# Attention beside two MLPs on one core: the low part of the row maxima by way of PSUM, and the broadcast of reciprocal sums in two transfers

## The chip, the cores and the metric

One core of a Trainium2 chip runs the whole program. The metric is the device time of one execution in microseconds (us), the median of several runs. A core has TensorE (PE, matrix products), VectorE (DVE), ScalarE (ACT), GpSimd (POOL) and SyncE (SP, which issues DMA transfers). SBUF is the large on-chip memory; PE writes its results to PSUM.

## The reference

Three parts in a row: causal attention with a position bias for 4 batches of 8 heads (576 tokens, 64 columns each), a dense MLP, and a mixture of eight experts with capacity. The change touches attention alone:

```python
scores = scale * np.matmul(q, k.transpose(0, 1, 3, 2))
s_pos = np.maximum(s, 0.0)
cum = np.cumsum(s_pos, axis=-1)
bias = -(cum[:, :, :, None] - cum[:, :, None, :])
scores = np.where(causal, -1000000000.0, scores + np.minimum(bias, 0.0))
scores = scores - np.max(scores, axis=-1, keepdims=True)
attn = np.exp(scores)
attn = attn / (np.sum(attn, axis=-1, keepdims=True) + 1e-09)
return np.matmul(attn, v).astype(np.float32)
```

Then follow `x @ w_in`, a piecewise quadratic function, `@ w_out`; and top-1 routing of 2304 tokens to eight experts of 288 tokens, each `relu(x @ w1) @ w2`.

## The kernel before, in words

The order of the work is written by hand: each engine carries out its instructions in the order in which the program issues them.

**Attention** (class `Attention`) goes through 32 heads, two of which make a pair; an even and an odd head differ in what is prepared beside them. `run` (L383) does for head n: the maxima of the rows (`rows_max`, L236), the product of the previous head's weights with its values (`values`, L313), the scores again, transposed, with their exponentials (`exps`, L275), and pieces of the preparation of the next pair (`prep_hi`, `prep_lo`) and of the normalization of earlier pairs (`norm`, L361).

**The row maxima.** `rows_max` computes scores in six tiles of PSUM (tag "s", four buffers) by two matmuls each (L249, L250), and VectorE takes the negated maximum of each row (L252 with the causal mask, L256 without) into `mc`, 128 rows by five columns. The matmuls work on numbers of reduced precision, so every operand is split into a high part and a remainder. For the maxima this is `nm`: L258 casts `mc` to the high part, L259 subtracts it from `mc`, which gives the low part. `rows_put` (L262) transposes both on PE (L271, five small matmuls), and ScalarE copies them as two rows into the operand Z (L272); by these rows the second score product subtracts the maximum before the exponential. `rows_put` is called in the midst of `values` of the previous head: six values matmuls (L333) stand ahead of L271 on PE, four behind it, then the scores of `exps` (L301).

**Normalization.** V has a column of ones, so `values` yields the sums of the weights too. `sums` (L354) lays them out as 128x9, and `norm` goes in five steps: 0 adds 1e-9 and takes the reciprocals (L369, L370), 1 writes them to DRAM (`rd`, L372), 2 reads them back as a tile R in which 64 partitions for each of the pair's two heads hold the same 576 numbers (L375), 3 multiplies (L378), 4 stores (L381). The steps of a pair lie in heads after it: step 2 of a pair stands in one odd head, step 3 in the next odd head. The transfers are issued from GpSimd's queue (`self.q`); after attention, for the last pairs, from SP's.

**Beside it** VectorE, ScalarE and GpSimd convert the first MLP's weights, which come as 64-bit floats in two 32-bit words, in every head (`narrow`, L486): VectorE takes the words apart (L495, L496, L501, L503), ScalarE converts (L499, L505), and GpSimd multiplies mantissa by exponent, two tiles in SBUF of 128x512 (L506). SP loads q, k and v for pairs to come (L187, L189, L178) and the raw weights (L514, L518).

**After attention** come the dense MLP (`Ffn`), routing (`Route`) and the experts (`Experts`). The first iterations of the MLP take weights that were converted before and carry out the last steps of `norm`.

Of the kernel before, what the change touches and what calls it, by code (L numbers as in the profile page):

```python
# [18 lines left out]
OP = mybir.AluOpType  # L19
# [5 lines left out]
def f(t):  # L25
    return t.bitcast(F32)
# [7 lines left out]
class Attention:  # L34
# [201 lines left out]
    def rows_max(self, n, fill):  # L236
        nc = self.nc
        X, Y, Z, W = self.stacks[(n // 2) % 2]
        h = n % 2
        mc = self.mcol[n % 2]  # L240
        for i, c0, c1, col in ((4, 0, 320, 5), (4, 320, 576, 4), (3, 0, 448, 3), (2, 0, 320, 2),
                               (1, 0, 192, 1), (0, 0, 64, 0)):
            if i == 1:
                fill()
            t = self.ps.tile([128, 512], F32, name="ps", tag="s", bufs=4)
            a, b = self.QT[i]
            m, w = b - a, c1 - c0
            diag = c1 == b
            nc.tensor.matmul(t[:m, :w], X[:, h, a:b], Y[:, h, c0:c1], start=True, stop=False)  # L249
            nc.tensor.matmul(t[:m, :w], Z[:96, h, a:b], W[:96, h, c0:c1], start=False, stop=True)  # L250
            if c1 == b:
                nc.vector.tensor_tensor_reduce(t[:m, :w], t[:m, :w], self.ml[:m, 448 + m - w:448 + m], -1.0,  # L252
                                               mc[:m, 5:6] if i == 4 else 3e38, op0=OP.add, op1=OP.min,
                                               accum_out=mc[:m, col:col + 1])
            else:
                nc.vector.tensor_reduce(mc[:m, col:col + 1], t[:m, :w], axis=AX.X, op=OP.max, negate=True)  # L256
        nm = self.w.tile([128, 5, 2], F32R, name="nm")
        nc.vector.tensor_copy(nm[:, :, 0], mc[:, :5])  # L258
        nc.vector.tensor_tensor(nm[:, :, 1], mc[:, :5], f(nm)[:, :, 0], op=OP.subtract)  # L259
        return nm  # L260

    def rows_put(self, n, nm):  # L262
# [98 lines left out]
    def norm(self, p, step):  # L361

        if not 0 <= p < self.NP:
            return
        nc, S = self.nc, self.S
        u0, r9, x = self.done[p]
        n = 2 * p
        if step == 0:
            nc.vector.tensor_scalar(r9, r9, 1e-9, None, op0=OP.add)  # L369
            nc.vector.reciprocal(r9, r9)  # L370
        elif step == 1:
            self.q.dma_start(self.rd[n:n + 2].rearrange("h (p s) -> (h p) s", p=64), r9)  # L372
        elif step == 2:
            R = self.nw.tile([128, S], F32, name="R")
            self.q.dma_start(R, self.rd[n:n + 2, None, :].to_broadcast([2, 64, S]))  # L375
            self.done[p] = (u0, r9, R)
        elif step == 3:
            nc.vector.tensor_tensor(x, u0, x, op=OP.mult)  # L378
        else:
            b, hh = divmod(n, self.H)  # L380
            self.q.dma_start(self.xd[64 * hh:64 * hh + 128, b * S:(b + 1) * S], x)  # L381
# [1278 lines left out]
```

## Time and profile before

| what | value |
|---|---|
| median of 3 runs | 1036.65 us (1034.18 to 1041.91) |
| the profiled execution | 1032.85 us |
| its span in the trace | 1031.1 us, mean granted TensorE clock 0.981 |
| instructions | 18509 |
| attention | about 14 to 292 us of the span |

The profile is of one execution. Times are counted from the start of the span. Engines are busy with instructions of the program; DMA issues on an engine's queue are rows of the order of time too (SPq is SP's queue), and of the source of a line. PEld is the load of weights into PE, which runs beside PE. Matmuls are pipelined, so a row can begin before the one ahead of it ends. A row of the order of time is: start, length, engine, line, operation, output and inputs, shapes, number; in brackets the idle time of its engine before it and what ended it. A row that sums a stretch has the length, the busy time of PE, PEld, DVE, ACT and POOL with the number of instructions in brackets, the granted TensorE clock, the busy share of the 16 DMA engines, and what they moved in GB/s. In a source row, three numbers are the shortest, the median and the longest of one instruction in ns.

### The profile page before, as it was taken

How to read it: one execution, taken by the hardware profiler on the slowest of the kernel's cores; microseconds unless marked ns; L12 is line 12 of the kernel's file. 1: busy time of each engine (PE TensorE's matmuls, PEld its weight loads, DVE VectorE, ACT ScalarE, POOL GpSimd, SP SyncE). 2: the span in 40 equal slices, each digit the busy share in tenths (PEclk: the TensorE clock that was granted, in tenths of full speed). 3: DMA queues.
4: the chain of work that ended last, by engine and by line, in shares of the span. 5: the costliest groups of instructions: out<-in, count | busy, mean ns of one | idle time of the engine just before them, and what ended most of it. 6: DMA issues, size and time to landing. Idle time of an engine off the chain costs nothing.

```text
span 1031.1 us, 18509 instructions
## 1 busy us (share of the span) xinstructions
PE 964.3 (94%) x6479; PEld 854.7 (83%) x6479; DVE 768.1 (74%) x2109; ACT 490.2 (48%) x961; POOL 338.8 (33%) x391
## 2 busy tenths in 40 slices
PE   6899999999979999999999999999889978989995
PEld 5777777777767989899889898899789868979995
DVE  6688888878857669799999998875568777775410
ACT  5777777767745542332332323430345424546431
POOL 3144454534421000000000000330778858873211
PEclk9999999999989999999999999999999989999998
DMA  5768777776667140030121300102555436557300
GB/s 130 161 165 194 200 201 191 200 194 173 189 203 246 54 147 29 21 102 22 31 93 31 113 11 11 62 11 81 159 165 172 157 115 190 165 147 222 118 24 24
DMA packets 124347, 126.86 MB, mean 123 GB/s; under 512 B 74178, under 2 KB 90818, under 8 KB 124124
## 3 DMA queue, kind: packets, MB, share of 16 engines
q1 hardware_dynamic: 104604, 89.79, 30.7%
q0 software_dynamic: 18592, 34.75, 11.6%
q10 hardware_dynamic: 1056, 1.12, 0.4%
q8 instruction: 51, 0.84, 0.3%
q14 instruction: 44, 0.36, 0.1%
HBM read 93.55 MB, written 27.50 MB: 117 GB/s over the span
## 4 chain that ended last, share of the span: by engine, by line
PE 58%; DVE 24%; DMA 5%; issue 5%; ACT 5%; POOL 1%; SPq 1%; another core or an unknown queue 0%; POOLq 0%; ACTq 0%; DVEq 0%
PE py L1493 8%; PE ph L1441 8%; PE ph L620 8%; PE po L333 6%; PE pst L301 6%; DVE junk L682 6%; PE px L661 3%; PE px L663 3%; PE px L662 3%; ACT u L629 3%; PE ps L249 2%; PE ps L250 2%; DVE u L628 2%; DVE gl L642 2%; PE rp L1128 2%
## 5 line engine op out<-in xcount | busy, mean ns | idle before, releaser
L1219 POOL TENSOR_TENSOR wl<-raw,wh 128x512 fp32r<-128x512 f32 x98 | 129.2, 1345 | 57.7 <-DMA raw<-in_moe_w_dram 33.8
L629 ACT ACTIVATE u<-u,half 128x384 f32<-128x384 f32 x96 | 59.3, 617 | 173.8 <-DVE u L628 169.0
L620 PE MATMUL ph<-xh,ih 128*128 128x384 f32 x384 | 130.8, 341 | 3.6 <-ACT ih L584 3.6
L620 PE MATMUL ph<-xh,il 128*128 128x384 f32 x384 | 130.6, 340 | 0.2 <-DVE il L592 0.2
L620 PE MATMUL ph<-xl,ih 128*128 128x384 f32 x384 | 130.5, 340 | 0.0
L333 PE MATMUL po<-E,V 128*128 128x320 f32 (+4 forms) x448 | 113.9, 383 | 0.4 <-ACT E L305 0.4
L663 PE MATMUL px<-oh,gl 128*128 128x512 f32 x240 | 95.3, 397 | 3.7 <-DVE gl L642 3.7
L661 PE MATMUL px<-oh,gh 128*128 128x512 f32 x240 | 95.2, 397 | 1.9 <-ACT x L670 1.8
L662 PE MATMUL px<-ol,gh 128*128 128x512 f32 x240 | 94.5, 394 | 0.0
L333 PEld LDWEIGHTS po<-E,V 128*128 128x128 f32 (+1 forms) x448 | 75.9, 194 | 20.5 <-issue 7.8
L682 DVE SCALAR_TENSOR_TENSOR junk<-x,gb 128x512 f32<-128x512 f32 x120 | 84.9, 737 | 4.5 <-ACT x L670 4.5
L682 DVE SCALAR_TENSOR_TENSOR junk<-wt,gb 128x512 f32<-128x512 f32 x128 | 82.9, 685 | 0.0
L1493 PE MATMUL py<-hh,wh 128*128 128x288 f32 x256 | 81.0, 317 | 0.0
L1219 ACT ACTIVATE wh<-raw 128x512 fp32r<-128x512 f32 x128 | 75.9, 624 | 9.2 <-DMA raw<-in_moe_w_dram 8.0
L1441 PE MATMUL ph<-xh,wh 128*128 128x288 f32 x256 | 79.4, 310 | 0.4 <-ACT xh L1219 0.4
L1441 PE MATMUL ph<-xl,wh 128*128 128x288 f32 x256 | 79.0, 309 | 0.5 <-DVE xl L1219 0.4
L620 PEld LDWEIGHTS ph<-xh,ih 128*128 128x128 f32 x384 | 72.7, 189 | 8.0 <-ACT ih L584 3.9
L1441 PE MATMUL ph<-xh,wl 128*128 128x288 f32 x256 | 78.4, 306 | 0.0
L1493 PE MATMUL py<-hl,wh 128*128 128x288 f32 x256 | 77.5, 303 | 0.0
L1493 PE MATMUL py<-hh,wl 128*128 128x288 f32 x256 | 77.2, 302 | 0.0
L620 PEld LDWEIGHTS ph<-xl,ih 128*128 128x128 f32 x384 | 72.7, 189 | 3.4
L506 POOL TENSOR_TENSOR co<-cm,ce 128x512 f32<-128x512 f32 x32 | 40.5, 1264 | 104.2 <-ACT cm L505 99.4
(228 smaller groups left out, 2487.9 us busy)
## 6 DMA issues: line engine op xcount, KB each, us to landing
raw<-in_moe_w_dram SPq DMA_DIRECT2D x128, 256.0 KB
r<-in_moe_w_in_dram SPq DMA_DIRECT2D x16, 512.0 KB
r<-in_moe_w_out_dram SPq DMA_DIRECT2D x16, 512.0 KB
xg<-xd SPq DMA_DIRECT2D x6, 768.0 KB
x2d<-x SPq DMA_DIRECT2D x36, 128.0 KB
Y<-Y POOLq DMA_DIRECT2D x15, 288.0 KB
nk<-in_k_dram SPq DMA_DIRECT2D x32, 128.0 KB
nq<-in_q_dram SPq DMA_DIRECT2D x32, 128.0 KB
```

What stands on the lines that cost most here:

```text
L301: nc.tensor.matmul(pst[u][:, cols], l, r, start=first, stop=last, skip_group_check=u == "c" or u == "b")
L333: nc.tensor.matmul(t[:, 256 + c0:256 + g1], V[:b - a, kb, 64 * h:64 * h + 128], E[:b - a, e0:e0 + g1 - c0], start=i == 0, stop=i == len(or ...
L506: nc.gpsimd.tensor_tensor(out, f(m), f(e), op=OP.mult)
L620: nc.tensor.matmul(p[:, :G], a[:, s], b, start=n == 0, stop=n == 11)
L629: nc.scalar.activation(u, u, AF.Square, bias=self.half, scale=0.5)
L661: nc.tensor.matmul(px[t][:, cols], gh[:, s], oh[:, cols], start=i == 0, stop=False)
L662: nc.tensor.matmul(px[t][:, cols], gh[:, s], ol[:, cols], start=False, stop=False)
L663: nc.tensor.matmul(px[t][:, cols], gl[:, s], oh[:, cols], start=False, stop=last)
L682: self.nc.vector.scalar_tensor_tensor(junk, x(), 1.0, self.gb[:, e], op0=OP.mult, op1=OP.mult, accum_out=out[:, e:e + 1])
L1219: return fn(*a, **kw)
L1441: self.nc.tensor.matmul(p[:, :self.C], a[:, cols], b, start=c == 0 and i == 0, stop=c == 3 and i == 2)
L1493: nc.tensor.matmul(p[:, :C], a[:, o:o + 128], b[:, fb], start=fb == 0 and i == 0, stop=fb == 7 and i == 2)
```

## The change

Two edits. In `rows_max`, `mc` is copied to five unused columns of the last score tile in PSUM, and the subtraction that yields the low part reads `mc` from there. In step 2 of `norm`, the one transfer with the source [2, 64, 576] becomes two with the source [64, 576], one for each head, to the two halves of R's partitions.

```diff
@@ -256,7 +256,10 @@
         nm = self.w.tile([128, 5, 2], F32R, name="nm")
         nc.vector.tensor_copy(nm[:, :, 0], mc[:, :5])
-        nc.vector.tensor_tensor(nm[:, :, 1], mc[:, :5], f(nm)[:, :, 0], op=OP.subtract)
+
+
+        nc.vector.tensor_copy(t[:, 256:261], mc[:, :5])
+        nc.vector.tensor_tensor(nm[:, :, 1], t[:, 256:261], f(nm)[:, :, 0], op=OP.subtract)
         return nm
 
     def rows_put(self, n, nm):
@@ -372,7 +375,9 @@
         elif step == 2:
             R = self.nw.tile([128, S], F32, name="R")
-            self.q.dma_start(R, self.rd[n:n + 2, None, :].to_broadcast([2, 64, S]))
+
+            for h in range(2):
+                self.q.dma_start(R[64 * h:64 * h + 64], self.rd[n + h:n + h + 1, :].to_broadcast([64, S]))
             self.done[p] = (u0, r9, R)
```

## Rows read from the trace of the kernel before

**Rows 1.** The page, busy time, share of the span and instructions of each engine.

```profile
PE 964.3 (94%) x6479; PEld 854.7 (83%) x6479; DVE 768.1 (74%) x2109; ACT 490.2 (48%) x961; POOL 338.8 (33%) x391
```

**Rows 2.** By stretch: length, busy PE, PEld, DVE, ACT, POOL, clock, DMA share, GB/s.

```profile
234.25:242.75 8.50, 7.78 (x53) 6.16 (x53) 8.13 (x21) 6.25 (x13) 5.19 (x7) 1.00 0.83 206
242.75:251.12 8.37, 8.37 (x56) 6.78 (x55) 6.42 (x22) 6.56 (x14) 2.85 (x5) 1.00 0.74 187
206.25:217.18 10.93, 9.04 (x54) 7.33 (x53) 6.54 (x22) 7.37 (x14) 2.59 (x5) 0.87 0.60 165
```

**Rows 3.** Order of time, an odd head: around the maxima's low part.

```profile
233.17 1.86 PE L333 MATMUL po<-E,V 128*128 128x320 f32 x6
...
234.25 0.17 DVE L258 CAST nm<-m 128x5 fp32r<-128x5 f32 x1
234.41 1.26 POOL L506 TENSOR_TENSOR co<-cm,ce 128x512 f32<-128x512 f32 x1 [4.11 <-ACT cm L505]
234.46 1.24 DVE L259 TENSOR_TENSOR nm<-m,nm 128x5 fp32r<-128x5 f32 x1
...
235.75 0.52 PE L271 MATMUL pr<-identr,nm 64*2 64x64 f32 x5 [0.72 <-DVE nm L259]
```

**Rows 4.** Order of time, an earlier odd head: the same instructions.

```profile
44.40 1.86 PE L333 MATMUL po<-E,V 128*128 128x320 f32 x6
...
45.68 0.17 DVE L259 TENSOR_TENSOR nm<-m,nm 128x5 fp32r<-128x5 f32 x1
45.69 1.29 POOL L506 TENSOR_TENSOR co<-cm,ce 128x512 f32<-128x512 f32 x1 [4.72 <-issue]
...
46.19 0.52 PE L271 MATMUL pr<-identr,nm 64*2 64x64 f32 x5
```

**Rows 5.** Order of time, an even head: low part and transposes.

```profile
242.95 0.17 DVE L259 TENSOR_TENSOR nm<-m,nm 128x5 fp32r<-128x5 f32 x1
...
243.87 0.52 PE L271 MATMUL pr<-identr,nm 64*2 64x64 f32 x5
```

**Rows 6.** Order of time, VectorE: first and last of 12 long subtractions.

```profile
61.76 1.24 DVE L259 TENSOR_TENSOR nm<-m,nm 128x5 fp32r<-128x5 f32 x1
...
268.20 1.24 DVE L259 TENSOR_TENSOR nm<-m,nm 128x5 fp32r<-128x5 f32 x1
```

**Rows 7.** Source of L259, and who on PE waited for it (us, times).

```profile
L259 DVE TENSOR_TENSOR nm<-m,nm x32: 165/167/1251, 14.5 to 284.4; 128x5 fp32r<-128x5 f32 x32
...
  PE pr L271: 9.6, 13
```

**Rows 8.** Groups by line and shape: small VectorE operations that read PSUM.

```profile
L737 DVE COPY L<-plt 128x24 f32<-128x24 f32 x1 | 0.2, 182 | 1.6 <-PE plt L735 1.6
...
L252 DVE CUSTOM_DVE_ANT_0 ps<-ps,ml 64x64 f32<-64x64 f32 x32 | 8.2, 255 | 0.0
```

**Rows 9.** Order of time, another odd head: GpSimd, a masked maximum, the cast.

```profile
216.68 1.26 POOL L506 TENSOR_TENSOR co<-cm,ce 128x512 f32<-128x512 f32 x1 [5.82 <-ACT cm L505]
...
216.83 0.26 DVE L252 CUSTOM_DVE_ANT_0 ps<-ps,ml 64x64 f32<-64x64 f32 x1
...
217.18 0.79 DVE L258 CAST nm<-m 128x5 fp32r<-128x5 f32 x1
```

**Rows 10.** Source of L375: GpSimd's issues of the broadcast.

```profile
L375 POOL DMA_DIRECT2D R<-rd x14: 835/848/1072, 65.8 to 288.0; - x14
```

**Rows 11.** By stretch, the MLP's begin: loads, then one of SP's broadcasts.

```profile
298.00:300.00 2.00, 0.00 (x0) 0.00 (x0) 0.00 (x0) 0.00 (x0) 0.00 (x0) 0.91 1.04 402
...
306.00:308.00 2.00, 1.24 (x5) 0.79 (x4) 1.97 (x7) 0.00 (x0) 0.00 (x0) 0.88 0.13 49
```

**Rows 12.** Order of time: a broadcast, a load of q, and PE's wait.

```profile
201.16 0.85 POOL L375 DMA_DIRECT2D R<-rd  x1
...
201.46 0.63 SPq L187 DMA_DIRECT2D nq<-in_q_dram  x1
...
212.59 0.24 PE L196 MATMUL pt<-identf,nq 64*128 64x64 f32 x1 [1.89 <-DMA nq<-in_q_dram]
```

## The prediction

> **What bounds the kernel now.** I read the page first, then the sums by stretch, then the order of time around the changed lines, and last the sources of single lines. The page has TensorE busy for 94% of the span [rows 1]: time is won only where PE stands still, or where what it works on becomes less. The change takes no work from PE, so I looked for PE's idle time beside the touched lines. Attention works in heads of two kinds. An even head takes 8.37 us, all of it PE; an odd head takes 8.50, of which PE is busy for 7.78 [rows 2]. The 0.72 us that are missing stand at one place in the order of time: PE ends its values matmuls at 235.03 (233.17 + 1.86) and begins the transposes of the row maxima (L271) at 235.75, released by the subtraction that the change touches (L259) [rows 3]. That subtraction works on 128x5 numbers and took 1.24 us. It began at 234.46, 0.05 after a GpSimd multiplication of two SBUF tiles (L506, 234.41, 1.26 long), and ended 0.03 after it. In another odd head the same subtraction began 0.01 before the GpSimd operation; it took 0.17 us, and PE did not wait: L271 began 0.07 before the last values matmul ended [rows 4]. So the 1.07 us are no work, they are a wait for GpSimd. It happens in 12 odd heads, the first at 61.76 and the last at 268.20 [rows 6]; the shortest subtraction is 165 ns, the median 167, the longest 1251 [rows 7].
>
> **Part 1, the low part from PSUM.** Removed: a subtraction with two SBUF inputs. Added: a copy of five columns from SBUF to PSUM, and a subtraction with one input in PSUM and one in SBUF. Does the new subtraction wait for GpSimd? The nearest row with one input in PSUM and one in SBUF, running inside a GpSimd operation, is the masked maximum of 64x64 at 216.83: 0.26 us there, inside 216.68 to 217.94 [rows 9], and 255 ns is its mean over all heads [rows 8]. So it isn't held, and I take it that the new one isn't either.
>
> No row has a copy from SBUF to PSUM beside a GpSimd operation. The Trainium skill (SBUF — State Buffer, "Who interferes with whom") says that a VectorE instruction with at most one SBUF input, outside the two-port modes, does not contend with GpSimd, and that the two-port modes are for SBUF to SBUF; by it the copy is not held, and the sum below stands. No run here shows it yet.
>
> The price: a copy of 128x24 out of PSUM takes 182 ns, and the 64x64 operation 255 [rows 8]; for five columns I take 0.19 each and a step of 0.21 from one to the next, as from the cast to the subtraction now (234.25 to 234.46) [rows 3]. Counted from the first of the last six values matmuls, the subtraction begins at 1.28 in the undisturbed head (45.68 - 44.40) and L271 at 1.79 (46.19 - 44.40) [rows 4]. With the change the copy begins at 1.28, the subtraction at 1.49, it ends at 1.68, and 0.04 later (235.70 to 235.75 [rows 3]) PE may start, at 1.72. That is ahead of 1.79, so in the 12 held heads L271 moves from 2.58 (235.75 - 233.17) to 1.79: 0.79 us each, 9.5 in all. Should both cost 0.26 with 0.04 between, PE starts at 1.28 + 0.26 + 0.04 + 0.26 + 0.04 = 1.88, and 0.70 us are left, 8.4 in all. More than 0.79 isn't there, since PE itself is late next: its values matmuls.
>
> What the added copy costs elsewhere: 32 x 0.21 = 6.7 us of VectorE. In odd heads VectorE has 8.13 busy of 8.50, of which 1.07 go; 7.27 of 7.7 remain. In even heads it becomes 6.63 of 8.37 [rows 2], and there the subtraction ends at 243.12, 0.75 before L271 begins [rows 5]: covered. Only where PE waits for the maxima without GpSimd in the way does it show. PE waited 13 times, 9.6 us [rows 7]; 12 x 0.72 is 8.6, so one head more (the first, which has no values to multiply) waits some 1.0: plus 0.2 there. Queued behind on VectorE are the low parts of the next pair and the normalization; in odd heads they come 0.85 earlier, in even heads 0.21 later, and no row shows PE waiting for them in those heads. The PSUM tile is now held until the subtraction. A head takes 12 tiles of that tag from 4 buffers, and the next user of this one is a score tile whose matmul stands behind L271 on PE, which waits for the subtraction anyway: no new wait.
>
> **Part 2, one broadcast for each head.** 16 transfers become 32; 14 pairs are issued by GpSimd, the last two by SP. An issue takes GpSimd 848 ns now [rows 10]; two cost between the same in all and twice that, so 0 to 0.85 us more for each pair. GpSimd is busy for 5.19 of 8.50 and 2.85 of 8.37 [rows 2]; behind it stand the store of an earlier pair and the next multiplication, which has this slack. I take nothing. SP's two extra issues stand ahead of loads that are issued iterations ahead: nothing.
>
> The transfer itself: while one of SP's broadcasts runs nearly alone, the DMA share is 0.13 of 16 engines, 2.1 engines, at 49 GB/s [rows 11]. Its 128 x 576 x 4 bytes take 6.0 us at that rate. Spread over all engines, at the 402 GB/s of another row [rows 11], 0.7. Nobody waits for it: it is used in the next odd head, 16.9 us later [rows 2]. What can change is whom it holds up on its two engines. One head took 10.93 instead of 8.37 us, with the granted clock at 0.87 [rows 2]; in it PE waited 1.89 for the last load of q, issued 0.30 behind such a broadcast [rows 12]. Ends: such a wait more, 2.6 us lost, or the whole excess gone, 2.6 won. I take the 1.9 of the wait itself, since those two issues stand so close. After attention PE stands still around 298 to 300 for a weight load, but there all engines are full (1.04, 402 GB/s [rows 11]): evening out gives nothing; the bound is the 2.0 us of that row.
>
> Two rules of the Trainium skill bear on it (DMA: Bandwidth & Descriptors). "Rules for kernel authors" says of two transfers to disjoint partition halves not to bother, they serialize: by that, part 2 gives nothing. "Why a DMA increments its semaphore by 16 and not by 1" says that the number of engines must divide the slowest dimension of both patterns, which is the 2 of this source: by that, two engines before and 16 after, as the 0.13 has it. I hold with the second.
>
> **The sum.** 9.5 - 0.2 + 1.9 = 11.2 us. The profiled execution took 1032.85 (span 1031.1, and 1.75 around it), so 1021.65 by its own measure. It lies 3.8 below the median of the three timed runs, 1036.65 (1034.18 to 1041.91); carried over, 1025.4.
>
> **The rivals.**
> First: the transfers change nothing (the load waits for another one, or the shared engines aren't what holds it). For it: the head of 10.93 is one of 32. Then 9.3 us: 1027.3.
> Second, the other side: GpSimd holds an instruction ahead of the subtraction. The cast before it can be held: at 217.18 it took 0.79 instead of 0.17, and it ended 0.03 after the GpSimd operation [rows 9]. In the held heads the cast begins 0.16 before GpSimd [rows 3]; from there on it decides: if GpSimd comes over 0.16 earlier against VectorE, the cast waits, and copy and subtraction follow it: the low part comes 0.42 later than now. 12 x 0.42 + 0.2 is 5.2 us: 1041.9. If the copy is the one that is held, 0.21 x 12 + 0.2: 1039.4. Against it: both engines follow PE, whose order up to this place doesn't change, and the first and the last of the 12 took the same 1.24 [rows 6], so GpSimd's start keeps its place against the subtraction.
> Third: shorter heads leave loads less time, and a head like that of 10.93 comes once or twice more: 9.3 less 2.6 to 5.2, 1030.0 to 1032.5.
> Fourth: it doesn't do what it says, because another wait stands right behind on PE, such as the copies of the transposed maxima by ScalarE: 1036.65. Against it: in the undisturbed odd head PE runs on without one [rows 4].
>
> **The numbers.** Forecast 0.42, first rival 0.33, third 0.12, second 0.08, fourth 0.05. One per cent, about what a measurement of this kernel can tell from no change, is 10.4 us: below 1026.3 lies most of the forecast (0.8 of it), some of the first rival by the scatter of runs (0.4), little of the third: 0.49 faster. Slower by more than 1% takes two mishaps at once, 0.04; the rest, 0.47, is within. The range goes from 1018.5 (9.5 + 2.6 + 2.0 = 14.1 won, and the 3.8 by which one execution lies under the median) to 1036.0, which takes in the third rival and leaves out the second and fourth.
>
> **What would show it.** L259 at 0.2 us in every head, also while L506 runs; a copy of some 0.19 before it; odd heads at 7.7 to 7.8 us; PE's waits for L259 down to the first head's; the 64-row broadcasts done in under 1 us, with no stretch at 0.13. Wrong it would be if the cast or the copy took 1.2 us in odd heads, if L271 still waited, or if heads of 10 us were more than one.

## The result and the profile after

The changed kernel takes 1025.76 us (median of 6 runs, 1024.51 to 1029.28), the kernel before, run beside it, 1038.56 (6 runs, 1034.18 to 1042.40): the ratio is 0.9874 with a 95% interval of 0.9847 to 0.9901, or 12.8 us between the medians. In a second comparison, on another chip, it was 0.9898 [0.9865, 0.9930].

The page of the changed kernel, its span and the busy times that answer to [rows 1]:

```profile
span 1022.8 us, 18581 instructions
PE 962.5 (94%) x6479; PEld 856.1 (84%) x6479; DVE 764.5 (75%) x2141; ACT 489.9 (48%) x961; POOL 341.2 (33%) x405
```

TensorE is again at 94%: the span became 8.3 us shorter, and 6.5 of them are time in which PE no longer stands still (1031.1 - 964.3 = 66.8 before [rows 1], 1022.8 - 962.5 = 60.3 now). Where that was is seen in the order of time of an odd head, as in [rows 3]:

```profile
220.66 1.86 PE L336 MATMUL po<-E,V 128*128 128x320 f32 x6
...
221.75 0.17 DVE L258 CAST nm<-m 128x5 fp32r<-128x5 f32 x1
221.83 0.16 DVE L261 COPY ps<-m 128x5 f32<-128x5 f32 x1
221.90 1.27 POOL L511 TENSOR_TENSOR co<-cm,ce 128x512 f32<-128x512 f32 x1 [4.09 <-ACT cm L510]
222.02 0.17 DVE L262 TENSOR_TENSOR nm<-ps,nm 128x5 fp32r<-128x5 f32 x1
...
222.46 0.52 PE L274 MATMUL pr<-identr,nm 64*2 64x64 f32 x5
```

The subtraction (now L262) begins 0.12 inside GpSimd's multiplication (now L511) and takes 0.17 us. L274, the former L271, begins 1.80 after the first of the six values matmuls (222.46 - 220.66), before the last of them ends at 222.52, and PE's row has no wait. The step from the cast to the subtraction is 0.27 (222.02 - 221.75). The source of the subtraction, which answers to [rows 7], says that this holds in every head, and that PE waited for it once:

```profile
L262 DVE TENSOR_TENSOR nm<-ps,nm x32: 164/165/167, 14.5 to 269.4; 128x5 fp32r<-128x5 f32 x32
...
  PE pr L274: 1.1, 1
```

The sums by stretch of the changed kernel: an odd and an even head, then attention, the MLP's begin (to its second group of matmuls), and the experts. Columns as in [rows 2].

```profile
221.75:229.22 7.47, 7.47 (x52) 6.01 (x51) 7.11 (x21) 6.13 (x13) 5.33 (x7) 1.00 0.65 131
229.22:237.83 8.61, 8.61 (x57) 6.93 (x56) 6.51 (x23) 6.68 (x15) 2.90 (x5) 1.00 0.83 245
0.00:276.80 276.80, 264.22 (x1696) 212.06 (x1696) 223.07 (x704) 209.68 (x404) 129.53 (x191) 0.99 0.74 192
276.80:352.80 76.00, 70.36 (x340) 61.69 (x341) 50.11 (x91) 38.29 (x70) 5.62 (x8) 0.98 0.46 148
...
709.10:1008.70 299.60, 273.08 (x2440) 260.26 (x2438) 184.68 (x513) 130.01 (x283) 174.48 (x165) 0.95 0.46 138
```

The same three stages of the kernel before (attention, the MLP's begin, the experts):

```profile
0.00:291.90 291.90, 268.13 (x1695) 213.90 (x1696) 235.88 (x672) 210.13 (x404) 126.75 (x177) 0.99 0.72 181
291.90:370.90 79.00, 71.47 (x340) 62.59 (x341) 50.16 (x91) 38.30 (x70) 5.60 (x8) 0.96 0.45 146
...
727.50:1019.50 292.00, 269.73 (x2439) 256.21 (x2438) 175.29 (x513) 129.78 (x283) 176.04 (x166) 0.97 0.46 142
```

Both heads of a pair are now all PE, 7.47 + 8.61 = 16.08 us against 8.50 + 8.37 = 16.87 [rows 2]: 0.79 less. Attention is 15.1 us shorter, the MLP's begin 3.0. The experts, which the change doesn't touch, are 7.6 longer in this pair of executions, at a clock of 0.95 instead of 0.97. That is taken as the scatter of executions, since the kernel before, traced once more, had attention end at 289.0 and took 299.7 for the experts:

```profile
0.00:289.00 289.00, 266.84 (x1695) 213.40 (x1696) 235.16 (x672) 209.96 (x404) 127.36 (x177) 0.99 0.72 183
...
724.60:1024.30 299.70, 275.00 (x2439) 262.30 (x2438) 184.23 (x513) 130.09 (x283) 176.96 (x166) 0.94 0.46 138
```

So the two profiled executions, 1032.85 and 1024.55, differ by only 8.3, and the medians by 12.8. Attention is 12 to 15 us shorter, by which execution of the kernel before one takes, but that takes in the first heads, which differ from one execution to the next. A narrower stretch, from the cast (L258) of the sixth head, the first in which the subtraction was held, to that of the last head, is this in the second trace of the kernel before, with the transfers alone (an experiment below), and in the changed kernel:

```profile
62.80:281.32 218.52, 208.98 (x1368) 166.96 (x1368) 187.44 (x530) 164.70 (x325) 104.30 (x142) 1.00 0.74 191
...
59.33:277.91 218.58, 209.05 (x1368) 166.99 (x1368) 187.35 (x531) 164.58 (x325) 106.67 (x155) 1.00 0.73 193
...
60.77:269.12 208.35, 208.10 (x1368) 167.17 (x1368) 175.23 (x557) 164.59 (x325) 106.22 (x155) 1.00 0.76 202
```

The first trace of the kernel before has 222.67 there (61.56 to 284.23). Its second has no head like that of 10.93, and no engine in it waits for a load between 40 and 276. Against its 218.5 the changed kernel wins 10.2, which is 13 held subtractions at 0.79 (the second trace had 13 of them, the first 12), and the MLP's begin, 79.0 in either trace of the kernel before, gives 3.0 more: together 13.2, about the 12.8 of the medians.

### The profile page after: what moved, and what is told of

Read it like the earlier page. It is cut to its first block, busy times and chain, and to the rows that moved or that the text cites. A ratio compares the mean times of both kernels' runs of the same rounds, so it can differ in the third digit from the quotient of the medians.

```text
span 1022.8 us, 18581 instructions
## 1 busy us (share of the span) xinstructions
PE 962.5 (94%) x6479; PEld 856.1 (84%) x6479; DVE 764.5 (75%) x2141; ACT 489.9 (48%) x961; POOL 341.2 (33%) x405
## 3 DMA queue, kind: packets, MB, share of 16 engines
q0 software_dynamic: 12544, 34.70, 11.2%
## 4 chain that ended last, share of the span: by engine, by line
PE 65%; DVE 20%; ACT 5%; issue 4%; DMA 2%; POOL 1%; SPq 0%; ACTq 0%; POOLq 0%; DVEq 0%
PE po L336 10%; PE py L1498 9%; PE ph L1446 8%; PE ph L625 8%; PE pst L304 6%; DVE junk L687 6%; PE px L666 3%; PE px L668 3%; PE px L667 3%; ACT u L634 3%; PE ps L249 3%; PE ps L250 2%; DVE gl L647 2%; DVE u L633 2%; PE rp L1133 2%
## 5 line engine op out<-in xcount | busy, mean ns | idle before, releaser
L666 PE MATMUL px<-oh,gh 128*128 128x512 f32 x240 | 95.4, 397 | 2.4 <-ACT x L675 1.4
L714 POOL DMA_DIRECT2D wt<-w32o x16 | 8.8, 549 | 195.0 <-DVE junk L687 195.0
```

The costliest lines, as they stand in the source:

```text
L666: nc.tensor.matmul(px[t][:, cols], gh[:, s], oh[:, cols], start=i == 0, stop=False)
```

## The experiments

The theory after the result: the subtraction is held because it has two inputs in SBUF while GpSimd reads SBUF, and undoing that wins some 9 us; the transfers win the 2 to 4 that are left. The rival: the two edits hang together, or the transfers do it all. Line numbers in a fence are those of the kernel whose trace it shows: an added line moves them by a few. Ratios are to the kernel before on the same chip.

**One edit alone.** The first keeps the one transfer, the second the subtraction from SBUF.

```diff
+        nc.vector.tensor_copy(t[:, 256:261], mc[:, :5])
-        nc.vector.tensor_tensor(nm[:, :, 1], mc[:, :5], f(nm)[:, :, 0], op=OP.subtract)
+        nc.vector.tensor_tensor(nm[:, :, 1], t[:, 256:261], f(nm)[:, :, 0], op=OP.subtract)
```

```diff
-            self.q.dma_start(R, self.rd[n:n + 2, None, :].to_broadcast([2, 64, S]))
+            for h in range(2):
+                self.q.dma_start(R[64 * h:64 * h + 64], self.rd[n + h:n + h + 1, :].to_broadcast([64, S]))
```

> The kernel before with the first edit alone (the low part from the copy in PSUM); the broadcast stays one transfer. Theory (the first edit removes GpSimd's hold on the subtraction in 12 odd heads, the second frees transfers): the subtraction takes 0.17 us in every head, a pair of heads 16.1 us instead of 16.9, and 9 to 10 us of the 12.8 us go: a ratio of 0.990 to 0.992. Heads of 10 us by a late load still come. Rival (the transfers give nothing of their own): the whole of it, 0.987. Rival (the transfers are most of it): 0.995 or more.

> The kernel before with the second edit alone (a broadcast for each head); the subtraction keeps its two inputs in SBUF. Theory: the subtraction still takes 1.24 us in some 12 odd heads and a pair 16.9 us; a broadcast lands in 3 to 4 us instead of 8 to 10, no head takes over 10 us, and 2 to 4 us go: a ratio of 0.996 to 0.998. Rival (nobody waits for what the broadcast holds up): 1.000.

Measured: the PSUM edit alone 1.0021 [0.9990, 1.0052], nothing; the transfers alone 0.9955 [0.9933, 0.9978], 4.7 us, with 2.3 to 7.0 in the interval; both 0.9874. The 9 to 10 us expected of the PSUM edit didn't come. The parts don't add up: with the transfers split, the PSUM edit is worth 0.9955 - 0.9874 = 0.0081, 8.4 us, give or take some 3.6 (an estimate from the two intervals), or 10.2 by the stretch above; without, nothing. Yet it did what it should. The source of its subtraction with the PSUM edit alone:

```profile
L260 DVE TENSOR_TENSOR nm<-ps,nm x32: 164/165/166, 14.6 to 284.4; 128x5 fp32r<-128x5 f32 x32
```

The waits of PE and VectorE in the same kernel, between 40 and 276 (us in total, times, the longest):

```profile
PE pt L196 <- DMA nq<-in_q_dram: 6.5, 2, 6.0
...
DVE ce L496 <- DMA r<-in_moe_w_in_dram: 4.0, 5, 1.3
DVE ce L496 <- DMA r<-in_moe_w_out_dram: 3.2, 1, 3.2
```

Subtractions of 0.17 throughout, but loads now come late: PE waited 6.5 us for q, VectorE 7.2 for raw weights. Undisturbed pairs are as short as in the changed kernel; others give it back, and the stretch from the sixth head's cast to the last's takes 222.24 (61.84 to 284.08), as in the first trace of the kernel before and 13.9 more than in the changed kernel. The trace is of the fastest of this kernel's 12 executions. Its sums by stretch, two heads and a later one:

```profile
144.30:151.78 7.48, 7.48 (x52) 6.01 (x52) 7.11 (x22) 6.12 (x13) 5.14 (x6) 1.00 0.75 179
151.78:160.38 8.60, 8.60 (x57) 6.92 (x56) 6.50 (x22) 6.67 (x15) 2.86 (x5) 1.00 0.86 219
...
169.29:185.18 15.89, 9.88 (x55) 8.16 (x54) 6.77 (x22) 7.38 (x14) 2.67 (x5) 0.79 0.56 157
```

One head took 15.89 us, and attention ends at 291.8, as before. What preceded that head's wait is the pattern of [rows 12]; its order of time, with an issue on SP that followed:

```profile
163.86 0.84 POOL L376 DMA_DIRECT2D R<-rd  x1
...
164.57 0.63 SPq L187 DMA_DIRECT2D nq<-in_q_dram  x1
...
169.28 6.30 SPq L515 DMA_DIRECT2D r<-in_moe_w_in_dram  x1
...
179.74 0.34 PE L196 MATMUL pt<-identf,nq 64*128 64x64 f32 x1 [6.00 <-DMA nq<-in_q_dram]
```

The load of q was issued 0.71 behind a broadcast, and PE had it 15.2 us after its issue (179.74 - 164.57). And SP stood 6.30 in an issue that otherwise takes 0.37. The sources of the issues of the first kind of raw loads (`in_moe_w_in_dram`) and of the broadcast, with the landing times of their issues, by kernel: the PSUM edit alone,

```profile
L515 SPq DMA_DIRECT2D r<-in_moe_w_in_dram x16: 367/420/6298, 18.5 to 273.6; - x16
...
DMA to landing us min/median/max: 4.9/13.8/14.3
...
L376 POOL DMA_DIRECT2D R<-rd x14: 835/850/1017, 65.3 to 287.8; - x14
...
DMA to landing us min/median/max: 10.1/11.4/12.0
```

and the changed kernel:

```profile
L519 SPq DMA_DIRECT2D r<-in_moe_w_in_dram x16: 367/374/604, 18.5 to 258.6; - x16
...
DMA to landing us min/median/max: 4.7/6.0/7.4
...
L380 POOL DMA_DIRECT2D R<-rd x28: 520/527/536, 64.3 to 273.4; - x28
...
DMA to landing us min/median/max: 2.8/3.2/7.4
```

One broadcast in one transfer lands after 11.4 us, in two after 3.2; these raw loads land after 13.8 and 6.0, at most 14.3 and 7.4. With the transfers alone they land after 4.5 to 5.5 us and PE waits for no load, while 13 subtractions are still long (PE waits 9.3 us for them between 40 and 276). Late loads by themselves cost little where heads are long: in the next experiment, with one transfer and pairs of 16.87 as before, the same loads land after 13.4 us in the median, and VectorE waits 0.8 for them in all. The rival holds: the edits hang together.

**Is it the copy, or the timing it brings?** The copy is made and nobody reads it; the subtraction reads SBUF as before, the broadcast is one transfer.

```diff
         nc.vector.tensor_copy(nm[:, :, 0], mc[:, :5])
+        nc.vector.tensor_copy(t[:, 256:261], mc[:, :5])
         nc.vector.tensor_tensor(nm[:, :, 1], mc[:, :5], f(nm)[:, :, 0], op=OP.subtract)
```

> The kernel before with the copy to PSUM added, and nobody reading it: the subtraction keeps its two inputs in SBUF. Theory (it is the two SBUF inputs that GpSimd holds): the subtraction still takes 1.2 us in odd heads, if a little less since it starts 0.1 to 0.2 later within the GpSimd operation; ratio 1.000 within 0.002. Rival (the copy moves the subtraction out of GpSimd's way in time, and what it reads doesn't matter): the subtraction takes 0.17 us and the ratio is 0.990.

Measured 1.0010 [0.9974, 1.0047]. Source of its subtraction:

```profile
L260 DVE TENSOR_TENSOR nm<-m,nm x32: 166/167/1246, 14.4 to 280.8; 128x5 fp32r<-128x5 f32 x32
```

The long subtractions are all there, 13 of them, and PE waited 14 times, 10.3 us, for L260. So it is the second input in SBUF, not the moment at which the subtraction comes; and the copy by itself costs nothing that can be measured.

**How is the transfer to be cut?** Two transfers again, but each a half of the columns, for both heads.

```diff
-            for h in range(2):
-                self.q.dma_start(R[64 * h:64 * h + 64], self.rd[n + h:n + h + 1, :].to_broadcast([64, S]))
+            for c in (slice(0, S // 2), slice(S // 2, S)):
+                self.q.dma_start(R[:, c], self.rd[n:n + 2, None, c].to_broadcast([2, 64, S // 2]))
```

> The changed kernel, but the two transfers of a broadcast are two halves of the columns, each for both heads, as the source [2, 64, 288]: as many transfers as in the change, and still a slowest dimension of 2. Theory (the number of engines is what counts): the broadcast takes 8 us or more to land, as before the change, and the time is that of the first edit alone, 0.990 to 0.992. Rival (two transfers instead of one are what helps): 0.987, as the change.

Measured 0.9851 [0.9811, 0.9890], as good as the change, though each source still has 2 as its slowest dimension and lands late; its source row of the broadcast:

```profile
L377 POOL DMA_DIRECT2D R<-rd x28: 822/837/857, 61.8 to 271.2; - x28
...
DMA to landing us min/median/max: 6.2/8.8/11.1
```

The forecast, the time of the first edit alone, missed. Attention from the sixth head's cast to the last's takes 208.34, as in the change (208.35), and neither PE nor VectorE waits for a load there. So within attention the landing time of the broadcast is not what counts, and the reason that I gave (two engines against sixteen) isn't needed. Nor is it the number of packets: the queue that carries GpSimd's transfers (q0 of the page) moved 18816 of them here, 18592 in the kernel before and 12544 in the changed one. At the MLP's begin the column halves win less, 78.1 us against 79.0 before and 76.0 in the change. Two shorter pieces may let others in between, hold them for a shorter time, or lie on different engines; which, no run here tells.

**The suspected cost, added.** To the changed kernel a broadcast of the same bytes is added for each pair, into a tile that nobody reads: once in one transfer, once in two.

```diff
             for h in range(2):
                 self.q.dma_start(R[64 * h:64 * h + 64], self.rd[n + h:n + h + 1, :].to_broadcast([64, S]))
+            R2 = self.nw.tile([128, S], F32, name="R2", bufs=1)
+            self.q.dma_start(R2, self.rd[n:n + 2, None, :].to_broadcast([2, 64, S]))
```

```diff
             for h in range(2):
                 self.q.dma_start(R[64 * h:64 * h + 64], self.rd[n + h:n + h + 1, :].to_broadcast([64, S]))
+            R2 = self.nw.tile([128, S], F32, name="R2", bufs=1)
+            for h in range(2):
+                self.q.dma_start(R2[64 * h:64 * h + 64], self.rd[n + h:n + h + 1, :].to_broadcast([64, S]))
```

> The changed kernel, and behind the two broadcasts of a pair a third one into a tile that nobody reads, written as before the change (source [2, 64, 576], one transfer). Theory (what counts is that one broadcast holds two of the engines for 7 us, and loads whose share lies on these engines land late): the raw weight loads take up to 10 us and more to land again, PE waits for loads of q or VectorE for raw weights, and the time goes back towards that of the first edit alone: a ratio of 0.995 to 1.003. Rival (the change helps by something else, such as the time at which R is there): 0.987, as the change.

> The changed kernel, and behind the two broadcasts of a pair the same bytes once more into a tile that nobody reads, as two transfers of 64 rows. Theory (engines held, not bytes): as the change, 0.985 to 0.991, loads land in 4 to 7 us. Rival (bytes): as the kernel with the third broadcast in one transfer.

Measured 1.0125 [1.0052, 1.0198] for the one, 0.9882 [0.9811, 0.9953] for the two: the same bytes cost 25 us more in one piece than in two (1054.59 - 1029.51, the medians), and in two next to nothing against the changed kernel's 0.9874. Waits with the one extra transfer, 40 to 276:

```profile
PE ps L249 <- DMA Y<-Y: 13.6, 8, 2.8
...
DVE ce L502 <- DMA r<-in_moe_w_in_dram: 5.2, 3, 3.3
...
POOL R L380 <- DMA rd<-r: 20.1, 9, 2.7
```

That is more than the 0.995 to 1.003 that I expected. PE, VectorE and GpSimd wait for other transfers than the added one; with the two extra transfers PE waits for no load. So the form of the transfer, not its bytes, holds up the others.

**A wait found on the way.** At the MLP's begin PE waits in the changed kernel 4.3 us for the low part of its first gate. Here that low part is begun first.

```diff
                 if g == 0:
+                    self.gl()
+                    self.gl = lambda: None
                     first(i)
```

> The changed kernel, and in the first group of the MLP VectorE computes the low part gl of an iteration ahead of that iteration's leftovers from attention (weight conversion, the last normalizations) instead of behind them. PE waited 4.3 us for gl there, 2.6 of them at one place, and some 3.4 us of half clock follow. Theory (that wait ends at VectorE's order alone): 2 to 5 us less than the change, a ratio to the kernel before of 0.983 to 0.985. Rival (the leftovers' loads and stores become late, or PE waits for the next weight instead): 0.987.

Measured 0.984 [0.978, 0.990], not to be told from the change. PE's waits for that low part, from the end of attention to the second group, first the changed kernel's:

```profile
PE px L668 <- DVE gl L647: 4.3, 3, 2.6
```

then with the low part first:

```profile
PE px L668 <- DVE gl L647: 2.7, 4, 1.1
```

Of the 1.6 us by which this wait became shorter, 1.1 came back at the neighbouring matmul (L666 for ScalarE's gh, 2.0 instead of 0.9), and the stage is no shorter (76.3 us against 76.0). The two that came out lowest, together, and the change beside them as a measure:

> The two edits that came out lowest, together: the broadcast as two transfers by columns, and the low part of the MLP's first gate begun earlier. Theory (the first is worth what the changed kernel's split is, and the second only moves a wait within the MLP's first group): no better than the changed kernel run beside it, ratio to before 0.984 to 0.988. Rival (each is worth some 2 us of its own): ratio 0.981 to 0.983, 4 us under the changed kernel.

> The changed kernel again, unchanged, beside the one with two transfers by columns and the earlier low part, as its measure: ratio to before 0.985 to 0.990. SP's issues of the raw loads all under 0.7 us again, the subtraction 0.17 in all 32 heads.

Measured 0.9878 [0.9836, 0.9919] and 0.9898 [0.9865, 0.9930]: no better version came out of this. In the changed kernel's second trace the subtraction again takes 0.17 in all 32 heads, and no issue of a raw load takes over 0.61 us.

**What GpSimd holds.** The change's own copy starts just ahead of GpSimd (0.07 in the head above), so it doesn't show whether a copy would be held. Two more copies that nobody reads, behind the subtraction, lie inside:

```diff
         nc.vector.tensor_tensor(nm[:, :, 1], t[:, 256:261], f(nm)[:, :, 0], op=OP.subtract)
+        nc.vector.tensor_copy(t[:, 264:269], mc[:, :5])
+        x = self.w.tile([128, 5], F32, name="mx", bufs=1)
+        nc.vector.tensor_copy(x, mc[:, :5])
```

> Behind the changed kernel's subtraction VectorE copies the same five columns of SBUF once more to PSUM, and then to a tile in SBUF; nobody reads either. In odd heads both then lie inside GpSimd's multiplication (in the changed kernel the subtraction is at 222.02 to 222.19, the multiplication at 221.90 to 223.17), where the change's own copy never lay wholly. Theory (an instruction with one input in SBUF and its output in PSUM is not held): the copy to PSUM takes 0.16 us in all 32 heads. Rival (GpSimd holds any reader of SBUF that meets it): it takes up to 0.9 in some 13 odd heads. The copy from SBUF to SBUF is open: 0.16 if only two inputs in SBUF are held, some 0.7 if input and output count alike; held or not, it stands behind the low part, so the time stays within 1 per cent of the changed kernel's 1025.8.

Order of time in an odd head:

```profile
212.95 1.26 POOL L514 TENSOR_TENSOR co<-cm,ce 128x512 f32<-128x512 f32 x1 [3.89 <-ACT cm L513]
...
213.27 0.17 DVE L263 COPY ps<-m 128x5 f32<-128x5 f32 x1
213.34 0.90 DVE L265 COPY mx<-m 128x5 f32<-128x5 f32 x1
```

The sources of both copies:

```profile
L263 DVE COPY ps<-m x32: 166/167/168, 14.3 to 280.4; 128x5 f32<-128x5 f32 x32
...
L265 DVE COPY mx<-m x32: 161/246/958, 14.4 to 280.5; 128x5 f32<-128x5 f32 x32
```

That odd head and the even one after it, by stretch:

```profile
212.79:221.39 8.60, 8.22 (x53) 6.27 (x53) 8.20 (x24) 6.26 (x13) 6.39 (x9) 1.00 0.58 160
221.39:229.73 8.34, 8.34 (x56) 6.75 (x55) 6.73 (x25) 6.57 (x14) 2.08 (x4) 1.00 1.05 259
```

From SBUF to PSUM no copy is held (168 ns at most); from SBUF to SBUF it ends 0.03 after GpSimd does (213.34 + 0.90, 212.95 + 1.26). The Trainium skill ("SBUF — State Buffer", Who interferes with whom) has both: one SBUF input outside the two-port modes doesn't contend, a copy in one of them does. The lengths here agree with it; which mode a copy ran in, no row shows. I had expected this kernel within 1% of the change, since the held copy stands behind the low part. That missed: its one execution took 1034.98, beside 1022.70 for the change, and the pair is 16.94 long instead of 16.08. L277 is no later for it (213.51, 0.72 behind the cast; 0.71 in the changed kernel), but all that VectorE does behind the copy is, and in the changed kernel's odd head VectorE has only 0.36 to spare (7.47 - 7.11). PE now waits for VectorE's maxima instead (L249 for L252, 3.1 us in 12 places between 40 and 290). So the price is not only PE's wait on the spot. How much of it is the hold, this run doesn't tell: VectorE's busy time in the odd head grew by 1.09 (8.20 - 7.11), of which the hold is some 0.73 (0.90 - 0.17) and the rest the copies' own length.

## Why the prediction was right, and where it was not

The time, 1025.4 against 1025.76, and the sum, 11.2 against 12.8, came out. That the time came so close is luck: 1.6 us more were won than forecast, and the kernel before, in six runs, stood 1.9 higher than in the three that I had counted from (1038.56 against 1036.65). And that the sum came out hangs on the edits being made together, as its parts show.

**The held subtraction: right.** The subtraction lies inside GpSimd's multiplication in 0.17 us, L274 starts at 1.80 where 1.79 was forecast, the pair lost 0.79, and PE waits once, 1.1 us, for the first head. In the company of the split transfers the edit is worth 8.4 us by the ratios and 10.2 by the stretch from the sixth head on, where 9.3 were forecast (9.5 - 0.2). The second rival (cast or copy held) and the fourth (another wait right behind) are out: cast and copy keep 0.17 and 0.16, but for one even head with 0.27 and 0.26 (the sources' longest, at 149.07), where PE doesn't wait.

**The copy's price: too high.** I took a step of 0.21 for it. The copy begins 0.08 after the cast, whose result it doesn't use, and the step from cast to subtraction grew from 0.21 to 0.27: 0.06. The sum hardly feels it, since the cover was there.

**The transfers: mis-sized.** I took 1.9, the wait for q in the one long head, with 2.6 as its upper end and 2.0 more after attention as a bound for the range. Alone they win 4.7. The step that failed is the sentence that after attention "evening out gives nothing", because all engines were full there. The kernel before had PE wait there for the MLP's weights, by its waits between 291 and 371:

```profile
PE ph L620 <- ACT ih L584: 3.6, 1, 3.6
```

In the changed one 0.2 is left of it, and with the transfers alone nothing. That the engines were full in one stretch of 2 us said nothing on when its loads could have landed: there too a broadcast had been issued shortly before (287.97), and ScalarE began on the first load of il 7.5 us after its issue (292.46, 300.01), against 4.1 in the changed kernel (277.34, 281.46). It was not all won, since PE then waits for the gate's low part; the stage went from 79.0 to 76.0, and to 76.2 with the transfers alone. In attention, where I had placed the 1.9, the transfers alone win 4.1 from the sixth head on against the first trace of the kernel before (222.67 - 218.58) and nothing against its second (218.52): a head like that of 10.93, with its stretch at a granted clock of 0.87 [rows 2], comes in some executions and not in others. In the changed kernel none from the fourth pair on is over 8.9. So the 1.9 stood for a wait that isn't always there, and the 2.8 to 3.0 that are came from a place that I had put at nothing.

**The edits are not independent: missed.** I added 9.5 and 1.9 as if each stood alone. The third rival (shorter heads leave loads less time) was given 0.12 and a loss of 2.6 to 5.2; for the PSUM edit alone it is true and takes everything, the 9.3 us forecast. In the changed kernel it is out, because the other edit gives the loads the time. The head of 10.93 was one of 32 in the first trace of before, and its second trace has none; with shorter heads such heads cost the whole gain (15.89 and 10.11 are the two longest of the later ones there).

**A sign that I named: wrong.** I wrote that 64-row broadcasts would be done in under 1 us. They land after 2.8 at the least, 3.2 in the median. Of the two rules of the Trainium skill that I weighed ("DMA: Bandwidth & Descriptors"), that of "Rules for kernel authors", not to bother with two halves, does not hold for this transfer: the measurements are 0.9955 [0.9933, 0.9978], and 1.0125 against 0.9882 for the same bytes added. The reason given there, that both halves use all 16 engines anyway, isn't met by one piece that keeps 2.1 of them busy [rows 11]. The rule of "Why a DMA increments its semaphore by 16 and not by 1" on how many engines divide a transfer, with which I held, fits the short landing of the 64-row form, but the column halves win as much in all with the dimension still 2: in attention it isn't what decides.

**GpSimd: as taken.** Two issues take 2 x 0.527 against 0.848 for one, 0.2 more for each pair, inside the 0 to 0.85; nobody waited for it.

**A slip in the range.** Its lower end, 1036.65 - 14.1 - 3.8, is 1018.75 and not 1018.5; nothing hangs on it.

## What to carry to other kernels

Two small edits are priced together where the first takes away the time in which the second's trouble was hidden: ask of each late transfer how late it is, and what becomes of it when the loop gets shorter. A transfer that lands after 11 us and that nobody waits for can still be a cost, if other queues' loads are issued behind it; look at the issue and landing of the loads (median and longest), not at who waits for the slow transfer itself. And where VectorE meets a GpSimd operation on SBUF, as here, an operand copied to PSUM frees a two-input instruction (0.17 instead of 1.24 us), while a copy from SBUF to SBUF is held as well (0.90).

## What was unexpected of the hardware

Where GpSimd issues the broadcast in one piece with a [2, 64, 576] source, SP's own issues stand: a raw load's issue, 367 to 374 ns at the shortest and in the changed kernel's median, took up to 6.30 us with the PSUM edit alone and 6.72 in the kernel before, and no more than 0.60 in the changed kernel. The rows of SP's issues in the order of time between 40 and 276 add up to 182 us of 236 in the kernel before, to 190 with the PSUM edit alone, and to 94 in the changed kernel (72, 72 and 73 rows). In the second trace of the kernel before the sum is 174, but the longest issue of a raw load 2.53; with column halves the sum is still 155 and the longest such issue 2.26; and in neither did VectorE wait for a raw load. So an issue that stands is a sign of the trouble and not its measure; what holds it inside the queue no row shows.
